# Products of the spectra in a long convolution: the order of two product pairs on VectorE, and of two spectrum stages on TensorE

## The chip, the cores and the metric

One Trainium2 chip, of which the kernel uses one core. Times are device microseconds of that core, as the median of several runs of the same kernel. A profile is one more execution, taken by the hardware profiler; its span runs from the first to the last instruction on the core.

## The reference

The program is a gated long convolution followed by two MLPs over 12480 tokens of 128 channels:

```python
u = x * v
L = 2 * S
Uf = np.fft.rfft(u, n=L, axis=1)
Hf = np.fft.rfft(h_filt, n=L, axis=0)
y = np.fft.irfft(Uf * Hf[None, :, :], n=L, axis=1)[:, :S, :]
return (x * y).astype(np.float32)
...
h = x @ w_in
g = np.where(h > 0.0, h, alpha * (np.exp(np.minimum(h, 0.0)) - 1.0))
return (g @ w_out).astype(np.float32)
...
h = x @ w_in
g = np.maximum(h, 0.0) + alpha * np.minimum(h, 0.0)
return (g @ w_out).astype(np.float32)
```

`h_filt` comes from a small MLP on position embeddings, times a decaying window. The change lies in `Uf * Hf`, the product of the two spectra.

## The kernel before, in words

The Fourier transforms are matrix products in two steps. The first (L239) leaves 99 residues of the input in `ureg` (view `a_u`) and of the filter in `sreg` (view `a_r`). The middle stage, the loop over `d` at L421 with 25 turns ("groups"; the program calls the group number d), finishes the transform of four residues a turn, multiplies the spectra and writes the products to DRAM (`yd`). Then comes the inverse transform (from L454 on) and the two MLPs, which take most of the time.

One group is made of these steps:
- `b_u(d)` (L337, TensorE): the spectrum of the input, 48 matmuls in the trace, into a PSUM tile of pool `psu` (name `pu`), which has two buffers. The products read it there, in PSUM.
- `b_h(d)` (L348, TensorE, 32 matmuls in the trace): the spectrum of the filter, from `rts[d % 2]`, into a tile of pool `psp` (name `ps`, two buffers). ScalarE copies it to SBUF (L351); that copy is `h`, two buffers.
- `b_r(d + 1)` (L319, TensorE, 32 matmuls): the residues of the next group's filter, also into a `psp` tile. ScalarE copies them to `rts[(d + 1) % 2]` with four copies (L323), which the next `b_h` reads.
- `products(d, u, h, 0, 2)` (L378). VectorE computes two large products of 128x1024, one for each pair of residues, e = 0 and e = 1 (L382); the small product `m2` of 128x512 for e = 1 (L385); the small product `mp` for e = 0, written over `u` in PSUM (L387); and the sum of `mp` into the tile of e = 0 (L388). GpSimd adds `m2` into the tile of e = 1 (L389) and then forms `y_sums`, two operations a pair (L371 and L372), first for e = 1, then for e = 0, into `ysts`. All five VectorE operations but L388 show at line L363, where `mul` stands.
- every second group, SyncE's queue writes the finished sums to DRAM (`y_write`, L400); each group it also loads the constants of the group three ahead (`load_g`, L271).

The large tiles come from `m_tile(True)` (L356): three slots of 1024 columns in `spreg`, taken in turn, so a group takes two and the slot that it takes first is the one after its predecessor's second. There is no scheduler: every engine runs its instructions in the order in which the program writes them, and waits for semaphores that the framework sets by tile regions. The last two groups, 23 and 24, compute only half of their products in the loop (`y1 == 1`) and the rest behind it (`late`, L440). Decoding of MLP weights (`dec_op`) is put between the groups by `run_hooks`: up to three extra VectorE operations of 128x512 a group, now and then one on ScalarE or GpSimd, in the first half of the loop only.

Of the kernel before, what the change touches and what calls it, by code (L numbers as in the profile page):

```python
# [13 lines left out]
ALU = mybir.AluOpType  # L14
# [32 lines left out]
def kernel(ctx: ExitStack, tc: tile.TileContext, posT, w1b, w2b, sc2, xva, xT,  # L47
                           fmat, fwin, gmat, wmat, finv, wi1, wo1, wi2, wo2, alphaT, out):
    nc = tc.nc
# [108 lines left out]
    def run_hooks(hooks, t):  # L158
        for x in sorted(hooks):
            if x <= t:  # L160
                for fn, args in hooks.pop(x):
                    fn(*args)
# [104 lines left out]
    def load_g(d):  # L267
        n = min(4, NF - 4 * d)
        o = 4096 + 4 * GWD * (d % 4)
        gts[d] = rreg[:, o : o + GWD * n].rearrange("p (f m) -> p f m", m=GWD)  # L270
        nc.sync.dma_start(gts[d], gmat[:, 4 * d : 4 * d + n, :])  # L271
# [32 lines left out]
    def fof(g, par):  # L304
        return min(2 * g + par, NF - 1)

    def rows(x):
        return slice(64 * x, 64 * x + 64)


    def b_r(d):
        ps = psp.tile([128, 1024], F32, name="ps")
        for e in range(2):
            for r in range(2):
                for par in range(2):
                    f = fof(2 * d + e, par)
                    for half in range(2):
                        c = par ^ half
                        nc.tensor.matmul(ps[rows(c), 512 * half + 128 * e : 512 * half + 128 * e + 128], a_r[rows(half), f, r],  # L319
                                         gts[d][rows(half), f - 4 * d, (64, 0)[r] : (192, 128)[r]], start=(r == 0), stop=(r == 1))  # L320
        for half in range(2):
            for par in range(2):
                nc.scalar.copy(rts[d % 2][rows(half), 256 * par : 256 * par + 256], ps[rows(par ^ half), 512 * half : 512 * half + 256])  # L323

    def b_u(d):
        ps = psu.tile([128, 1024], F32, name="pu")
        for e in range(2):
            for x in range(3):
                for par in range(2):
                    f = fof(2 * d + e, par)  # L330
                    for half in range(2):
                        o = 512 * half + 256 * e
                        a = a_u[rows(half), f]
                        src = (a.rearrange("k r w -> k (r w)"), a[:, 1], a[:, 0])[x]
                        dst = ps[rows(par), o + (0, 0, D)[x] : o + (2 * D, D, 2 * D)[x]]
                        g0 = (64, 0, 128)[x]
                        nc.tensor.matmul(dst, gts[d][rows(half), f - 4 * d, g0 : g0 + 64], src, start=(x == 0), stop=(x == 2))  # L337
        return ps.rearrange("k (h e r w) -> k h e r w", h=2, e=2, r=2)

    def b_h(d):  # L340
        ps = psp.tile([128, 1024], F32, name="ps")
        for e in range(2):
            for r in range(2):
                for par in range(2):
                    for half in range(2):
                        o = 512 * half + 256 * e + 128 * r
                        x = 256 * par + 128 * e + 64 * r
                        nc.tensor.matmul(ps[rows(par), o : o + D], rts[d % 2][rows(half), x : x + 64], w2_sb[rows(half)],  # L348
                                         start=True, stop=True)
        h = spreg[:, 4608 + 1024 * (d % 2) : 5632 + 1024 * (d % 2)]  # L350
        nc.scalar.copy(h.rearrange("k (e u w) -> k u e w", e=2, u=2), ps.rearrange("k (u e w) -> k u e w", u=2, e=2))  # L351
        return h.rearrange("k (e u r w) -> k e u r w", e=2, u=2, r=2)
# [3 lines left out]
    def m_tile(big):  # L356
        k = nm[big] % 3
        nm[big] += 1
        t = spreg[:, 1024 * k : 1024 * k + 1024] if big else spreg[:, 3072 + 512 * k : 3584 + 512 * k]
        return t.rearrange("k (r x w) -> k r x w", r=2, w=D)  # L360

    def mul(out, u, h, n):
        nc.vector.tensor_tensor(out, u.unsqueeze(2).to_broadcast([128, 2, n, D]), h.unsqueeze(1).to_broadcast([128, 2, n, D]), ALU.mult)  # L363

    def quarters(v):
        return v.rearrange("p y (h w) -> p y h w", h=NCH)

    def y_sums(g, m, y0, y1):
        q, e = divmod(g, 4)
        o = [ysts[q % 2][:, y0:y1, :, c, CH * e : CH * e + CH] for c in range(2)]  # L370
        nc.gpsimd.tensor_tensor(o[0], quarters(m[:, 0, 2 * y0 : 2 * y1 : 2]), quarters(m[:, 1, 2 * y0 + 1 : 2 * y1 : 2]), ALU.subtract)  # L371
        nc.gpsimd.tensor_tensor(o[1], quarters(m[:, 0, 2 * y0 + 1 : 2 * y1 : 2]), quarters(m[:, 1, 2 * y0 : 2 * y1 : 2]), ALU.add)  # L372

    def hx(h, e, u0, u1):
        return h[:, e, u0:u1].rearrange("k u r w -> k (u r) w")


    def products(d, u, h, y0, y1):  # L378
        n = 2 * (y1 - y0)
        ms = [m_tile(True) for e in range(2)]  # L380
        for e in range(2):
            mul(ms[e][:, :, 2 * y0 : 2 * y1], u[:, 0, e], hx(h, e, y0, y1), n)  # L382
        if y1 == 2:
            m2 = m_tile(False)
            mul(m2, u[:, 1, 1], hx(h, 1, 0, 1), 2)  # L385
            mp = u[:, 0].rearrange("k e r w -> k (e r w)").rearrange("k (r x w) -> k r x w", r=2, w=D)
            mul(mp, u[:, 1, 0], hx(h, 0, 0, 1), 2)  # L387
            nc.vector.tensor_tensor(ms[0][:, :, 2:4], ms[0][:, :, 2:4], mp, ALU.add)  # L388
            nc.gpsimd.tensor_tensor(ms[1][:, :, 2:4], ms[1][:, :, 2:4], m2, ALU.add)  # L389
        for e in (1, 0) if y1 == 2 else (0, 1):  # L390
            y_sums(2 * d + e, ms[e], y0, y1)

    def y_write(q, y0=0, y1=2):
        yst = ysts[q % 2][:, y0:y1].rearrange("p y h c w -> p (y h c) w")
        yv = yd[y0:y1].rearrange("y h (c k) w -> k (y h c) w", c=2)
        nfp = _fp_count(q)
        o = 8 * q * CH
        for par in range(2):
            nf = min(nfp, NF - 8 * q - nfp * par)
            nc.sync.dma_start(yv[:, :, o + par * nfp * CH : o + (par * nfp + nf) * CH],  # L400
                              yst[par * 64 : par * 64 + 64, :, : nf * CH])
# [19 lines left out]
    for d in range(ND):  # L421
        if d > 0 and d + 3 < ND:
            load_g(d + 3)
        run_hooks(hooks, 2 * d + 1)
        u = b_u(d)
        h = b_h(d)
        if d + 1 < ND:
            b_r(d + 1)
        if d > 1 and d % 2 == 0 and d < ND - 1:
            y_write(d // 2 - 1)  # L430
        if d < ND - 2:
            products(d, u, h, 0, 2)
        else:
            products(d, u, h, 0, 1)
            late.append((d, u, h))
# [4 lines left out]
    for d, u, h in late:  # L440
        products(d, u, h, 1, 2)
# [454 lines left out]
```

## Time and profile before

| | |
|---|---|
| time, median of 3 runs | 1517.39 us (1516.5 to 1523.01) |
| the profiled execution's own time | 1522.3 us |
| its span | 1520.5 us |
| TensorE matmul busy | 1430.0 us, 94% of the span |
| VectorE busy | 1282.5 us, 84% |
| ScalarE busy | 1087.5 us, 72% |
| GpSimd busy | 1019.3 us, 67% |
| mean granted TensorE clock | 0.985 of full speed |

The shares are means over stages with different limits. In the profile's forty slices of the span, TensorE's share is 9 tenths or more from the tenth slice (some 340 us) to the end and 6 to 8 tenths before it; the middle stage lies in the fourth to seventh slice, from about 117 to 277 us. PE means TensorE, PEld its weight loads, DVE VectorE, ACT ScalarE, POOL GpSimd, SP SyncE; the letter q behind a name is that engine's instruction queue.

### The profile page before, as it was taken

How to read it: one execution, taken by the hardware profiler on the slowest of the kernel's cores; microseconds unless marked ns; L12 is line 12 of the kernel's file. 1: busy time of each engine (PE TensorE's matmuls, PEld its weight loads, DVE VectorE, ACT ScalarE, POOL GpSimd, SP SyncE). 2: the span in 40 equal slices, each digit the busy share in tenths (PEclk: the TensorE clock that was granted, in tenths of full speed). 3: DMA queues.
4: the chain of work that ended last, by engine and by line, in shares of the span. 5: the costliest groups of instructions: out<-in, count | busy, mean ns of one | idle time of the engine just before them, and what ended most of it. 6: DMA issues, size and time to landing. Idle time of an engine off the chain costs nothing.

```text
span 1520.5 us, 25242 instructions
## 1 busy us (share of the span) xinstructions
PE 1430.0 (94%) x9143; PEld 1221.6 (80%) x9143; DVE 1282.5 (84%) x1817; ACT 1087.5 (72%) x2004; POOL 1019.3 (67%) x935
## 2 busy tenths in 40 slices
PE   7887666799999999999999999999999999999998
PEld 7886555788888888788888888888888888888887
DVE  5677776759898889888898898898888899988998
ACT  3444333467887777887888887878887888887884
POOL 4666776346678887888767666667666667666667
PEclk9999999899999999999999999999999999999999
DMA  8775687652012313222100400000000000000000
GB/s 257 222 259 143 158 236 197 200 160 82 19 45 59 87 49 87 69 76 83 50 8 18 195 25 24 24 7 18 24 24 24 25 7 17 25 24 21 7 7 13
DMA packets 98849, 116.89 MB, mean 77 GB/s; under 512 B 8518, under 2 KB 77834, under 8 KB 97560
## 3 DMA queue, kind: packets, MB, share of 16 engines
q1 hardware_dynamic: 95508, 104.19, 23.4%
q0 software_dynamic: 1296, 7.86, 1.5%
q10 hardware_dynamic: 1920, 3.21, 0.6%
q8 instruction: 72, 1.18, 0.3%
q14 instruction: 53, 0.43, 0.1%
HBM read 83.11 MB, written 32.15 MB: 76 GB/s over the span
## 4 chain that ended last, share of the span: by engine, by line
PE 67%; DVE 12%; POOL 8%; ACT 5%; issue 4%; DMA 4%; SPq 0%; POOLq 0%; ACTq 0%; DVEq 0%
PE psh L610 11%; PE psh L612 10%; PE psh L611 10%; PE pso L610 9%; PE pso L611 9%; PE pso L612 9%; PE psi L512 3%; DVE spreg L363 3%; DVE ureg L655 2%; PE pa L239 2%; POOL rreg L371 2%; POOL rreg L372 2%; POOL spreg L389 2%; PE ps L454 2%; DVE g1l L633 2%
## 5 line engine op out<-in xcount | busy, mean ns | idle before, releaser
L633 POOL TENSOR_TENSOR g2l<-ureg,g2h 128x490 fp32r<-128x490 f32 (+3 forms) x315 | 373.2, 1185 | 132.1 <-ACT g2h L684 63.5
L633 POOL TENSOR_TENSOR g1l<-ureg,g1h 128x486 fp32r<-128x486 f32 (+3 forms) x313 | 346.0, 1106 | 165.8 <-ACT g1h L661 159.7
L673 DVE TENSOR_SCALAR ureg<-psh,al_sb 128x486 f32<-128x486 f32 (+3 forms) x416 | 295.8, 711 | 83.7 <-PE psh L612 78.3
L647 ACT ACTIVATE ureg<-psh 128x490 f32<-128x490 f32 (+2 forms) x393 | 225.7, 574 | 114.1 <-PE psh L612 96.9
L678 DVE SCALAR_TENSOR_TENSOR ureg<-psh,ureg 128x486 f32<-128x486 f32 (+3 forms) x416 | 274.1, 659 | 14.3
L655 DVE SCALAR_TENSOR_TENSOR ureg<-ureg,psh 128x486 f32<-128x486 f32 (+3 forms) x416 | 268.1, 644 | 2.8 <-ACT ureg L648 2.0
L661 ACT CAST g1h<-ureg 128x490 fp32r<-128x490 f32 (+3 forms) x405 | 240.2, 593 | 17.8 <-DVE ureg L655 14.7
L648 ACT ACTIVATE ureg<-ureg 128x490 f32<-128x490 f32 (+2 forms) x393 | 239.7, 610 | 12.8
L684 ACT CAST g2h<-ureg 128x490 fp32r<-128x490 f32 (+3 forms) x404 | 234.6, 581 | 8.4 <-DVE ureg L678 6.8
L610 PE MATMUL psh<-x1h,wi1h 128*128 128x486 f32 (+3 forms) x416 | 169.7, 408 | 6.8 <-DVE ureg L655 3.9
L610 PE MATMUL psh<-x2h,wi2h 128*128 128x486 f32 (+3 forms) x416 | 158.6, 381 | 0.0
L611 PE MATMUL psh<-x2l,wi2h 128*128 128x486 f32 (+3 forms) x416 | 158.5, 381 | 0.0
L612 PE MATMUL psh<-x1h,wi1l 128*128 128x486 f32 (+3 forms) x416 | 158.3, 381 | 0.0
L612 PE MATMUL psh<-x2h,wi2l 128*128 128x486 f32 (+3 forms) x416 | 158.3, 381 | 0.0
L611 PE MATMUL psh<-x1l,wi1h 128*128 128x486 f32 (+3 forms) x416 | 158.2, 380 | 0.0
L611 PE MATMUL pso<-g2l,wo2h 128*128 128x490 f32 (+3 forms) x404 | 154.3, 382 | 0.6 <-POOL g2l L633 0.6
L610 PE MATMUL pso<-g1h,wo1h 128*128 128x490 f32 (+3 forms) x405 | 154.6, 382 | 0.3 <-ACT ureg L703 0.3
L611 PE MATMUL pso<-g1l,wo1h 128*128 128x490 f32 (+3 forms) x405 | 154.4, 381 | 0.2 <-POOL g1l L633 0.2
L612 PE MATMUL pso<-g1h,wo1l 128*128 128x490 f32 (+3 forms) x405 | 154.6, 382 | 0.0
L612 PE MATMUL pso<-g2h,wo2l 128*128 128x490 f32 (+3 forms) x404 | 154.1, 381 | 0.0
L610 PE MATMUL pso<-g2h,wo2h 128*128 128x490 f32 (+3 forms) x404 | 153.9, 381 | 0.0
L633 DVE TENSOR_TENSOR g1l<-ureg,g1h 128x490 fp32r<-128x490 f32 (+3 forms) x104 | 123.3, 1186 | 20.9 <-ACT g1h L661 10.3
(169 smaller groups left out, 2567.6 us busy)
## 6 DMA issues: line engine op xcount, KB each, us to landing
ureg<-yd SPq DMA_DIRECT2D x50, 256.0 KB
yd<-rreg SPq DMA_DIRECT2D x22, 512.0 KB
rreg<-in_gmat_dram SPq DMA_DIRECT2D x24, 384.0 KB
ureg<-in_finv_dram SPq DMA_DIRECT2D x23, 379.0 KB
ureg<-zd SPq DMA_DIRECT2D x4, 1584.0 KB
x<-in_xva_dram SPq DMA_DIRECT2D x32, 196.0 KB
v<-in_xva_dram SPq DMA_DIRECT2D x32, 196.0 KB
zd<-ureg SPq DMA_DIRECT2D x24, 256.0 KB
```

Of the source, the lines that this page charges most:

```text
L363: nc.vector.tensor_tensor(out, u.unsqueeze(2).to_broadcast([128, 2, n, D]), h.unsqueeze(1).to_broadcast([128, 2, n, D]), ALU.mult)
L610: nc.tensor.matmul(ps[:, :w], ah, bh[:, :w], start=start, stop=False)
L611: nc.tensor.matmul(ps[:, :w], ah, bl[:, :w], start=False, stop=False)
L612: nc.tensor.matmul(ps[:, :w], al, bh[:, :w], start=False, stop=stop)
L633: eng.tensor_tensor(lo[:, :w], e[:, :w], hi[:, :w], ALU.subtract)
L647: nc.scalar.activation(e[:, :w], ps[:, :w], AF.Relu, scale=-1.0)
L648: nc.scalar.activation(e[:, :w], e[:, :w], AF.Exp, scale=-1.0)
L655: nc.vector.scalar_tensor_tensor(e[:, :w], e[:, :w], -1.0, ps[:, :w], op0=ALU.add, op1=ALU.max)
L661: nc.scalar.copy(hi[:, :w], e[:, :w])
L673: nc.vector.tensor_scalar(e[:, :w], ps[:, :w], 0.0, al_sb[:, c : c + 1], op0=ALU.min, op1=ALU.mult)
L678: nc.vector.scalar_tensor_tensor(e[:, :w], ps[:, :w], 0.0, e[:, :w], op0=ALU.max, op1=ALU.add)
L684: nc.scalar.copy(hi[:, :w], e[:, :w])
```

## The change

Two things are written in another order; no operation is added or removed, and none changes its size.

```diff
     def products(d, u, h, y0, y1):
         n = 2 * (y1 - y0)
-        ms = [m_tile(True) for e in range(2)]
-        for e in range(2):
+        ms = {}
+
+        def first(e):
+            ms[e] = m_tile(True)
             mul(ms[e][:, :, 2 * y0 : 2 * y1], u[:, 0, e], hx(h, e, y0, y1), n)
+
+        first(1)
         if y1 == 2:
             m2 = m_tile(False)
             mul(m2, u[:, 1, 1], hx(h, 1, 0, 1), 2)
+            nc.gpsimd.tensor_tensor(ms[1][:, :, 2:4], ms[1][:, :, 2:4], m2, ALU.add)
+        y_sums(2 * d + 1, ms[1], y0, y1)
+        first(0)
+        if y1 == 2:
             mp = u[:, 0].rearrange("k e r w -> k (e r w)").rearrange("k (r x w) -> k r x w", r=2, w=D)
             mul(mp, u[:, 1, 0], hx(h, 0, 0, 1), 2)
             nc.vector.tensor_tensor(ms[0][:, :, 2:4], ms[0][:, :, 2:4], mp, ALU.add)
-            nc.gpsimd.tensor_tensor(ms[1][:, :, 2:4], ms[1][:, :, 2:4], m2, ALU.add)
-        for e in (1, 0) if y1 == 2 else (0, 1):
-            y_sums(2 * d + e, ms[e], y0, y1)
+        y_sums(2 * d, ms[0], y0, y1)
...
         run_hooks(hooks, 2 * d + 1)
+        h = b_h(d)
         u = b_u(d)
-        h = b_h(d)
         if d + 1 < ND:
             b_r(d + 1)
```

Since `m_tile` is now called for e = 1 first, the slots change hands too: the first slot of a group holds e = 1, the second e = 0.

On VectorE, the first two groups of the loop before (the two large products, x2, are e = 0 and e = 1; then `m2`, `mp` and the sum):

```order
L363 TENSOR_TENSOR spreg<-pu,spreg 128x1024 x2
L363 TENSOR_TENSOR spreg<-pu,spreg 128x512
L363 TENSOR_TENSOR pu<-pu,spreg 128x512
L388 TENSOR_TENSOR spreg<-spreg,pu 128x2x256
L363 TENSOR_TENSOR spreg<-pu,spreg 128x1024 x2
L363 TENSOR_TENSOR spreg<-pu,spreg 128x512
L363 TENSOR_TENSOR pu<-pu,spreg 128x512
L388 TENSOR_TENSOR spreg<-spreg,pu 128x2x256
```

and the same place in the changed kernel:

```order
L363 TENSOR_TENSOR spreg<-pu,spreg 128x1024
L363 TENSOR_TENSOR spreg<-pu,spreg 128x512
L363 TENSOR_TENSOR spreg<-pu,spreg 128x1024
L363 TENSOR_TENSOR pu<-pu,spreg 128x512
L396 TENSOR_TENSOR spreg<-spreg,pu 128x2x256
L363 TENSOR_TENSOR spreg<-pu,spreg 128x1024
L363 TENSOR_TENSOR spreg<-pu,spreg 128x512
L363 TENSOR_TENSOR spreg<-pu,spreg 128x1024
L363 TENSOR_TENSOR pu<-pu,spreg 128x512
L396 TENSOR_TENSOR spreg<-spreg,pu 128x2x256
```

The large product of e = 0 has moved behind `m2`; the rest stands as before.

On TensorE, from `b_r(0)` at the loop's entry through group 1 before (L337 is `b_u`, L348 `b_h`, L319 `b_r`; each row's matmul counts twice in the trace):

```order
L319 MATMUL ps<-rreg,sreg 64x128 x16
L337 MATMUL pu<-ureg,rreg 64x256 x4
L337 MATMUL pu<-ureg,rreg 64x128 x8
L337 MATMUL pu<-ureg,rreg 64x256 x4
L337 MATMUL pu<-ureg,rreg 64x128 x8
L348 MATMUL ps<-w_sb,rreg 64x128 x16
L319 MATMUL ps<-rreg,sreg 64x128 x16
L337 MATMUL pu<-ureg,rreg 64x256 x4
L337 MATMUL pu<-ureg,rreg 64x128 x8
L337 MATMUL pu<-ureg,rreg 64x256 x4
L337 MATMUL pu<-ureg,rreg 64x128 x8
L348 MATMUL ps<-w_sb,rreg 64x128 x16
```

and in the changed kernel:

```order
L319 MATMUL ps<-rreg,sreg 64x128 x16
L348 MATMUL ps<-w_sb,rreg 64x128 x16
L337 MATMUL pu<-ureg,rreg 64x256 x4
L337 MATMUL pu<-ureg,rreg 64x128 x8
L337 MATMUL pu<-ureg,rreg 64x256 x4
L337 MATMUL pu<-ureg,rreg 64x128 x8
L319 MATMUL ps<-rreg,sreg 64x128 x16
L348 MATMUL ps<-w_sb,rreg 64x128 x16
L337 MATMUL pu<-ureg,rreg 64x256 x4
L337 MATMUL pu<-ureg,rreg 64x128 x8
L337 MATMUL pu<-ureg,rreg 64x256 x4
L337 MATMUL pu<-ureg,rreg 64x128 x8
```

`b_h` now follows `b_r` directly, where `b_u` stood between them. ScalarE, GpSimd and SyncE's queue keep their order, but for the two half groups 23 and 24, whose sums GpSimd now forms for e = 1 first.

## Rows read from the trace of the kernel before

**Rows 1.** Windows: start and end, length, busy of five engines (instructions), clock, DMA share, GB/s.

```profile
117.00:262.00 145.00, 96.67 (x2548) 82.72 (x2552) 108.15 (x128) 59.24 (x124) 101.63 (x119) 0.91 0.69 183
...
300.00:1520.00 1220.00, 1207.79 (x5692) 1020.25 (x5691) 1072.61 (x1535) 964.17 (x1775) 842.57 (x744) 1.00 0.14 45
```

**Rows 2.** Chain that ended last, one group of the loop: start us, us, what.

```profile
251.30 1.83 DVE spreg L363 x2
253.27 1.28 POOL spreg L389
254.61 0.73 POOL rreg L371
256.71 0.70 POOL rreg L372
```

**Rows 3.** Timeline, VectorE and GpSimd: start, us, operation [idle before <- releaser].

```profile
251.30 1.82 DVE L363 TENSOR_TENSOR spreg<-pu,spreg 128x1024 f32<-128x1024 f32 x2 [1.72 <-POOL rreg L372]
...
253.16 0.70 DVE L363 TENSOR_TENSOR pu<-pu,spreg 128x512 f32<-128x512 f32 x1
253.27 1.27 POOL L389 TENSOR_TENSOR spreg<-spreg 128x512 f32<-128x512 f32 x1 [2.00 <-DVE spreg L363]
253.89 0.69 DVE L388 TENSOR_TENSOR spreg<-spreg,pu 128x512 f32<-128x512 f32 x1
254.50 1.22 DVE L363 TENSOR_TENSOR spreg<-pu,spreg 128x1024 f32<-128x1024 f32 x1
...
257.43 1.82 DVE L363 TENSOR_TENSOR spreg<-pu,spreg 128x1024 f32<-128x1024 f32 x2 [1.72 <-POOL rreg L372]
```

**Rows 4.** Timeline, TensorE and ScalarE, in the same group.

```profile
254.63 1.97 PE L337 MATMUL pu<-ureg,rreg 64*64 64x256 f32 x48 [2.42 <-DVE spreg L388]
...
256.42 1.05 PE L348 MATMUL ps<-w_sb,rreg 64*64 64x128 f32 x32
...
257.29 1.05 PE L319 MATMUL ps<-rreg,sreg 64*64 64x128 f32 x32
...
257.58 1.01 ACT L351 COPY spreg<-ps 128x1024 f32<-128x1024 f32 x1 [3.68 <-PE ps L348]
258.49 1.54 ACT L323 COPY rreg<-ps 64x256 f32<-64x256 f32 x4
```

**Rows 5.** Timeline, group 1: `b_h` behind ScalarE's four copies, then `b_r`.

```profile
117.35 1.54 ACT L323 COPY rreg<-ps 64x256 f32<-64x256 f32 x4
...
117.77 0.43 PE L348 MATMUL ps<-w_sb,rreg 64*64 64x128 f32 x2 [0.78 <-ACT rreg L323]
118.55 1.36 PE L348 MATMUL ps<-w_sb,rreg 64*64 64x128 f32 x29 [0.36 <-ACT rreg L323]
...
119.66 0.33 PE L319 MATMUL ps<-rreg,sreg 64*64 64x128 f32 x3
```

**Rows 6.** Timeline of TensorE around a fall of the clock; the fifth row is of the windows.

```profile
180.07 3.69 PE L337 MATMUL pu<-ureg,rreg 64*64 64x256 f32 x48 [3.03 <-DVE spreg L388]
...
183.53 1.93 PE L348 MATMUL ps<-w_sb,rreg 64*64 64x128 f32 x32
...
230.11 3.57 PE L337 MATMUL pu<-ureg,rreg 64*64 64x256 f32 x48 [2.42 <-DVE spreg L388]
233.44 1.19 PE L348 MATMUL ps<-w_sb,rreg 64*64 64x128 f32 x32
...
182.00:184.00 2.00, 2.00 (x40) 1.63 (x36) 0.71 (x1) 0.00 (x0) 1.25 (x2) 0.50 0.00 0
...
153.79 1.97 PE L337 MATMUL pu<-ureg,rreg 64*64 64x256 f32 x48 [3.22 <-DVE spreg L388]
```

**Rows 7.** Timeline: the first products of group 0 and of group 24.

```profile
117.54 2.95 DVE L363 TENSOR_TENSOR spreg<-pu,spreg 128x1024 f32<-128x1024 f32 x3 [1.29 <-ACT spreg L351]
...
266.46 3.08 DVE L363 TENSOR_TENSOR spreg<-pu,spreg 128x512 f32<-128x512 f32 x5 [2.22 <-ACT spreg L351]
```

**Rows 8.** Windows: the stretch of the loop in which the DMA engines are fullest.

```profile
184.00:216.00 32.00, 24.50 (x620) 21.13 (x612) 22.57 (x27) 13.31 (x28) 22.76 (x27) 0.86 0.94 255
```

## The prediction

> **What bounds the kernel now.** I read the windows first, to see which stage can gain. From 300 us on TensorE is busy 1207.79 of 1220 us: that part is full, and the change does not touch it. In the loop over the groups no engine is full: in 145 us VectorE works 108.15, GpSimd 101.63, TensorE 96.67 and ScalarE 59.24 [rows 1]. A stage in which nobody is full is held by a circle of waits, so the chain comes next. It goes round once a group: two VectorE products, GpSimd's L389, its four sums (of which the chain's rows show the outer two), and back to the products [rows 2]. The next turn begins at 257.43 [rows 3], 6.13 us after 251.30.
>
> The timeline says what closes the circle [rows 3]. VectorE runs the large product of e = 0 early (254.50), then idles 1.72 us until GpSimd's last L372 is done, and only then runs the large product of e = 1 and `m2` (257.43). That is the rotation of three slots: e = 1 takes the slot in which the group before had its e = 0, and GpSimd sums e = 0 last. GpSimd for its part idles 2.00 us for `m2`, which stands behind the blocked product. The sum along the circle: 1.83 for e = 1 and `m2`, 0.14 to GpSimd's start at 253.27, 1.34 to the first sum at 254.61, 2.82 for four sums: 6.13.
>
> TensorE and ScalarE lie beside this [rows 4]: `b_u` waits 2.42 us for VectorE to free its PSUM buffer, then `b_u`, `b_h`, `b_r` run through. The spectra are ready well before VectorE takes them.
>
> **The change, part by part.** *The products.* The group's first slot now holds e = 1, and its `m2` follows at once. The slot that e = 1 takes was last summed two groups earlier; the one that e = 0 takes held the e = 1 of the group before, which GpSimd sums first. So GpSimd's last sums are off VectorE's path. What is left is the work alone. VectorE: from 251.30 to the next group's e = 0 at 254.50 is 3.20, plus 1.15 for that product (1.22 less the overlap of consecutive rows): 4.35 us a group. GpSimd: from 253.27 to 257.42, 4.15 us [rows 3]. Nothing is added or lengthened: every GpSimd L389 and L371 here already runs beside VectorE's products. In the first half of the loop the decoding adds twelve operations of 128x512 on VectorE and six on GpSimd; at the 0.70 and 1.27 us of such operations here, 8 us over twelve groups on either, some 0.7 a group: 5.0 and 4.8 us.
>
> *The exchange of `b_h` and `b_u`.* This is what now sets the pace, I think. Before, `b_u(d+1)` stood between `b_r(d+1)` and `b_h(d+1)`, and covered ScalarE's four copies L323. Now `b_h` follows `b_r` directly and must wait for those copies; behind it on TensorE's queue wait `b_u` and the next `b_r`, and VectorE waits for `b_u`. A new circle: copies, `b_h`, `b_u`, `b_r`, copies. Its price is in the rows. Group 1 shows `b_h` behind the copies: its first two matmuls start at 117.77, the bulk from 118.55 with a last wait inside, and `b_r` follows at 119.66, that is 2.31 us after the copies began [rows 5]. From `b_u` to its successor 1.79, `b_r` 1.05, and 0.11 from TensorE's end to ScalarE's start (256.42 plus 1.05 to 257.58) [rows 4]: together 5.26. The bulk of that `b_r` started a tenth later; I take 5.3 us a group. ScalarE's L351 fits beside `b_u`, and `h` (copied while `b_u` runs) is ready before `u`. So the pace goes from 6.13 to 5.3, set by TensorE and ScalarE, not to VectorE's 4.35.
>
> *Where it begins and ends.* The copies of group 1 begin at 117.35 [rows 5] in both kernels: ScalarE's first L351 waits for transfers out of the memory that it overwrites. Group 24's copies then begin 23 x 5.3 = 121.9 us later, at 239.3; add 2.3 for `b_h`, 1.97 for `b_u` and a tenth: VectorE takes group 24 at 243.7, against 266.46 [rows 7]. That is **22.8 us** earlier. It counts the decoding's delays of today, which the slack of VectorE and GpSimd now swallows, and that group 24 no longer waits for `b_h` and L351 behind `b_u`. What comes behind (sums, write, load, inverse transform) keeps its order, and the full TensorE of the MLPs passes the gain on.
>
> *The clock.* Today a fall of the granted clock is free here; on the new circle it is not. Seven of the 23 `b_u` that begin between 121 and 261 us are long ones of 2.95 to 3.69 us, as at 180.07, where the row of windows grants 0.50, the 1.2 GHz level. All seven follow an idle gap of at least 2.42 us, but so do nine that stay at 1.97, one behind 3.22; none falls behind 1.10 or less [rows 6]. The new circle has a gap of about 1.7 us a group (copies and signals), which this trace does not show. Price of one fall: at 230.11 the successor starts 3.33 us later instead of 1.79, 1.5 us; at 180.07 it is 1.67 plus 0.88 on `b_h`, 2.55 us [rows 4, 6]; I take 2. Number of falls: from none to seven, as now; the gaps are shorter, so I take three, nearer to none. That takes 6 us: a gain of **16.8 us**.
>
> Edits costed at nothing: the half groups' order of pairs and the late products, which TensorE's and the DMA's work on the loop's end covers; without that cover, one half pair of sums, under 1 us. SyncE's queue keeps its order, and `load_g` still goes out some three groups ahead.
>
> The profiled execution took 1522.3 us, of which 1520.5 is span; less 16.8 is 1505.5. The median of the runs lies 4.9 below that execution, so I say 1500.6.
>
> **The rivals.**
> *A, the clock falls in most groups: slower.* TensorE is now on the path, with a gap in every group. If its clock falls in 20 of 23 groups, that costs 40 us against 22.8: 1517.4 + 17.2 = 1535. The gain is gone at 11 falls; from 15 or 16 on it is slower by 0.5%. For it: the gap recurs at each turn and a fall lengthens the very circle. Against it: the gaps are shorter than any that fell today, and TensorE's 3.7 us a group (1.79, 0.87 and 1.05) become a larger share of a shorter turn. A rule for it stands in the Trainium skill (TensorE: Matmul & The Clock Gate, A second HAM failure mode: psum-queue depth-cycling): a matmul engine that idles briefly between groups while PSUM buffers go round can swing between the two clock levels and lose throughput to it. By that rule the time would be this rival's; the trace agrees only in part, as gaps of 2.42 us fell in some groups and not in others. Chance 0.06.
>
> *B, the DMA engines hold part of it: smaller or no gain.* From 184 to 216 us they are 0.94 full [rows 8]. If those five groups keep their 6.13, 4 us are lost; if groups 11 to 24 all do, 14 x 0.83 = 11.6 us, which with the clock's three falls leaves a gain of 5: 1512. For it: the same bytes must pass in less time. Against it: over the loop the share is 0.69 [rows 1], 0.69 x 6.13 / 5.3 = 0.80, and loads go out three groups ahead. Chance of a gain under 7.6 us this way, or of a wait for GpSimd that stays (the slots not freed as I read them, then 1517): 0.09.
>
> *C, the new circle does not close* and VectorE's 4.35 sets the pace: 22 more us, 1478. Against it: `b_h` waits for ScalarE in group 1 already [rows 5]. Chance 0.04.
>
> **How the numbers follow.** My forecast, a gain of 8 to 23 us, has 0.81, C 0.04: faster by over 0.5% (7.6 us, about what a measurement of this kernel can tell from no change) 0.85; same 0.09; slower 0.06. The range: no fall and all of the 22.8 gives 1494.6, with a little for the pace 1493; seven falls of 2 us and 2 us of DMA waits leave 6.8, so 1510.6. 1493 to 1511.
>
> **What would show it.** In the changed kernel's trace: VectorE's and GpSimd's waits on each other nearly gone, VectorE's wait for `b_u` (L337) in their place; turns of 5.2 to 5.4 us at full clock, one or two us longer where the clock falls; TensorE's wait before L348 on ScalarE's L323; group 24 at about 244 to 252 us. I am wrong if VectorE still waits for L372, if turns of 5.3 do not appear at full clock, or if the clock is 0.50 in most groups.

## The result, and the profile after

The changed kernel takes 1499.79 us, the median of 4 runs (1498.55 to 1500.85), against 1518.72 us for the kernel before beside it (1516.50 to 1523.01). The ratio is 0.9871 (95% interval 0.9855 to 0.9887): 1.3% faster, clear of what the runs scatter. The forecast was 1500.6. Its profiled execution has a span of 1499.0 us, 21.5 less than the one before.

The time came from the loop over the groups, in which five engines now stand like this (windows: start and end, length, busy of PE, PEld, DVE, ACT and POOL with instructions, clock, DMA share, GB/s), beside [rows 1] and [rows 8]:

```profile
117.00:240.00 123.00, 101.85 (x2512) 83.00 (x2508) 105.10 (x124) 58.11 (x115) 100.13 (x119) 1.00 0.80 215
182.00:224.00 42.00, 34.94 (x860) 28.35 (x864) 32.18 (x38) 18.38 (x36) 32.32 (x40) 1.00 0.95 277
```

The clock is at its full level throughout the loop, where it was 0.91 of it on the mean, and the DMA engines' share went from 0.69 to 0.80. VectorE and GpSimd in the timeline of the changed kernel (start, us, operation, [idle before <- releaser]), which answers to [rows 3]:

```profile
224.43 2.95 DVE L363 TENSOR_TENSOR spreg<-pu,spreg 128x1024 f32<-128x1024 f32 x3 [1.00 <-PE pu L337]
...
226.33 1.27 POOL L390 TENSOR_TENSOR spreg<-spreg 128x512 f32<-128x512 f32 x1 [1.25 <-DVE spreg L363]
...
229.76 0.72 POOL L372 TENSOR_TENSOR rreg<-spreg 128x256 f32<-128x256 f32 x1
229.84 2.95 DVE L363 TENSOR_TENSOR spreg<-pu,spreg 128x1024 f32<-128x1024 f32 x3 [1.01 <-PE pu L337]
```

A turn lasts 5.41 us (224.43 to 229.84) instead of 6.13. VectorE runs its three products without a break and no longer waits for GpSimd's L372, which is still running when VectorE starts (229.76 and 229.84); it waits 1 us for `b_u` (L337). TensorE and ScalarE in the same turn answer to [rows 4]:

```profile
225.29 1.54 ACT L323 COPY rreg<-ps 64x256 f32<-64x256 f32 x4 [1.64 <-PE ps L319]
...
225.71 0.43 PE L348 MATMUL ps<-w_sb,rreg 64*64 64x128 f32 x2 [0.54 <-ACT rreg L323]
...
226.50 1.36 PE L348 MATMUL ps<-w_sb,rreg 64*64 64x128 f32 x29 [0.36 <-ACT rreg L323]
...
227.60 0.39 PE L337 MATMUL pu<-ureg,rreg 64*64 64x256 f32 x3
...
227.81 1.79 PE L337 MATMUL pu<-ureg,rreg 64*64 64x256 f32 x44
...
228.05 1.01 ACT L351 COPY spreg<-ps 128x1024 f32<-128x1024 f32 x1 [1.22 <-issue]
...
229.34 0.33 PE L319 MATMUL ps<-rreg,sreg 64*64 64x128 f32 x3
229.44 0.27 PE L337 MATMUL pu<-ureg,rreg 64*64 64x128 f32 x1
229.44 1.14 PE L319 MATMUL ps<-rreg,sreg 64*64 64x128 f32 x29
...
230.71 1.54 ACT L323 COPY rreg<-ps 64x256 f32<-64x256 f32 x4 [1.64 <-PE ps L319]
```

Read from top to bottom this is the circle: copies, `b_h` behind them, `b_u`, `b_r`, and the next copies 5.42 us later. The totals of waits from 117 to 240 us (engine, line <- whom: us, times, longest) say the same of the whole loop:

```profile
ACT rreg L323 <- PE ps L319: 38.1, 22, 2.4
PEld ps L348 <- ACT rreg L323: 34.7, 66, 0.8
...
DVE spreg L363 <- PE pu L337: 14.1, 14, 1.5
...
DVE spreg L363 <- POOL rreg L372: 1.8, 1, 1.8
```

The circle keeps its 5.41 us through the turns with decoding as well. VectorE's own turns there are up to 6.87 us long; it falls behind, catches up in later turns of down to 4.32 us, and does not hold TensorE.

Four turns were longer. In them TensorE stopped inside `b_r`, `b_h` or `b_u`, at an instruction for which the profile names no releaser, as here, where the copies came 6.2 us after the last ones:

```profile
136.27 0.66 PE L319 MATMUL ps<-rreg,sreg 64*64 64x128 f32 x14 [0.59 <-issue]
...
137.03 1.54 ACT L323 COPY rreg<-ps 64x256 f32<-64x256 f32 x4 [2.43 <-PE ps L319]
```

The others are at 199, 212 and 218 us. Together they cost 2.5 us. A second profiled execution of the changed kernel (`e8_change_again`, below) has none of them: its copies follow each other by 5.40 to 5.46 us in all 23 turns, with the DMA engines as full as here:

```profile
117.00:240.00 123.00, 102.88 (x2569) 84.89 (x2572) 106.87 (x127) 58.72 (x117) 102.04 (x120) 1.00 0.80 219
```

So full DMA engines alone do not make these stops. The profile's list of DMA queues (packets, MB, share) has a queue that, by its name, loads the engines' own code:

```profile
q8 instruction: 72, 1.18, 0.3%
```

In the packets that the trace keeps, each of the four stops ends 1.4 to 1.6 us after one of this queue's 16 KB packets was done (here 134.79, and 136.27 for the stop's end). The same holds for every such stop of 0.18 us or more in the loops of all twelve profiles of this case: 30 stops in six of them, 1.27 to 1.63 us after such a packet, while the packets come 3 to 13 us apart. That TensorE waited there for its own code is the reading that fits; no run changed the code's loading, so the cause is not shown.

The chain at the loop's end, in order of time:

```profile
246.08 0.70 DVE spreg L363
...
249.19 2.44 DMA yd<-rreg
...
251.84 2.87 DMA sreg<-yd
...
254.84 6.62 PE ps L460 x32
```

VectorE takes group 24 at 246.08, where it was 266.46 [rows 7], 20.4 us earlier. Eight to nine microseconds later the inverse transform begins, at 254.84; in the profile before it began at 275.26, the same 20.4. So the end of the loop and the MLPs passed on what they were given.

### The profile page after: what moved, and what is told of

Read it like the earlier page. It is cut to its first block, busy times and chain, and to the rows that moved or that the text cites. A ratio compares the mean times of both kernels' runs of the same rounds, so it can differ in the third digit from the quotient of the medians.

```text
span 1499.0 us, 25227 instructions
## 1 busy us (share of the span) xinstructions
PE 1432.3 (96%) x9143; PEld 1217.6 (81%) x9143; DVE 1279.1 (85%) x1817; ACT 1089.8 (73%) x2004; POOL 1019.6 (68%) x935
## 4 chain that ended last, share of the span: by engine, by line
PE 67%; DVE 8%; ACT 4%; issue 3%; POOL 1%; DMA 1%; POOLq 0%; SPq 0%; ACTq 0%; DVEq 0%
PE psh L616 11%; PE psh L618 10%; PE psh L617 10%; PE pso L616 10%; PE pso L617 10%; PE pso L618 10%; PE psi L518 3%; DVE ureg L661 2%; PE ps L460 2%; DVE g1l L639 2%; DVE ureg L679 1%; PE pu L460 1%; DVE ureg L684 1%; DVE g2l L639 1%; ACT ureg L654 1%
## 5 line engine op out<-in xcount | busy, mean ns | idle before, releaser
L667 ACT CAST g1h<-ureg 128x490 fp32r<-128x490 f32 (+3 forms) x405 | 240.3, 593 | 17.6 <-DVE ureg L661 14.1
```

The lines of the kernel that those rows point to most:

```text
L667: nc.scalar.copy(hi[:, :w], e[:, :w])
```

## The experiments

Every kernel ran beside the kernel before on its chip; ratios are to that. Three things were in question: whether the new circle sets the pace, what the exchange of `b_h` and `b_u` does, and which part of the products' new order opened the old circle.

**The products alone** (`e1_products_alone`): the change without its second part.

```diff
-        h = b_h(d)
         u = b_u(d)
+        h = b_h(d)
```

> Only the new order of the products, with b_u still ahead of b_h. Theory (the exchange makes the circle of copies, b_h, b_u, b_r that sets 5.41 us a turn in the changed kernel): without it VectorE's own 4.35 us sets the pace, about 5.0 while the decoding runs, so some 23 x 0.7 = 16 us less than the changed kernel, 1478 to 1490; VectorE's waits in the loop nearly gone. Rival (the exchange is needed, because b_u and b_h behind VectorE's free buffer bring h too late, above all where the clock falls): turns of 5.4 us or more, 1500 to 1515, with VectorE waiting for L351 in most groups.

Measured: 1490.6 us, ratio 0.9814 (0.9779 to 0.985). A second time, in one job with the changed kernel:

> The products alone once more. Theory (the exchange costs time): 6 to 12 us under the changed kernel beside it, 1488 to 1495. Rival (the first difference was the chip's): within 3 us of it.

> The changed kernel once more, beside the next two on one chip. Theory and rival alike: 1498 to 1504. Its profile tells whether the clock stays up in the loop in another execution: theory, no fall or one, since a turn of 5.41 us leaves short gaps; rival, falls come and go by chance, three or more.

Measured: 1493.09 us, 0.9828 (0.9811 to 0.9845), against 1498.6 us, 0.9860 (0.9843 to 0.9876), for the changed kernel. So the products alone are some 5 us better than the whole change beside it, and 9 by the medians of separate jobs; the intervals of the pair touch. The theory's direction holds and its size does not: the range of 1478 to 1490 was missed at its upper end, and beside the changed kernel the difference is 5.5 us where 6 to 12 were expected. The changed kernel's clock stayed at the full level in its second profile too, as the theory had it. The first profile of the products alone tells what took the rest. Its timeline:

```profile
118.48 2.94 DVE L363 TENSOR_TENSOR spreg<-pu,spreg 128x1024 f32<-128x1024 f32 x3
122.80 2.94 DVE L363 TENSOR_TENSOR spreg<-pu,spreg 128x1024 f32<-128x1024 f32 x3
...
131.77 2.94 DVE L363 TENSOR_TENSOR spreg<-pu,spreg 128x1024 f32<-128x1024 f32 x3
...
137.18 0.91 POOL L371 TENSOR_TENSOR rreg<-spreg 128x256 f32<-128x256 f32 x1
...
137.54 1.10 DVE L129 SCALAR_TENSOR_TENSOR ureg<-ureg 128x512 uint32<-128x512 uint32 x1
...
138.57 2.94 DVE L363 TENSOR_TENSOR spreg<-pu,spreg 128x1024 f32<-128x1024 f32 x3
...
198.70 1.10 PE L319 MATMUL ps<-rreg,sreg 64*64 64x128 f32 x32 [1.19 <-DMA rreg<-in_gmat_dram]
...
203.91 0.76 PE L348 MATMUL ps<-w_sb,rreg 64*64 64x128 f32 x18 [1.94 <-issue]
...
205.99 2.96 DVE L363 TENSOR_TENSOR spreg<-pu,spreg 128x1024 f32<-128x1024 f32 x3 [2.89 <-ACT spreg L351]
```

Without the exchange a bare turn (one without decoding) is 4.32 us (118.48 to 122.80), as VectorE's work asks: the exchange does cost 1.1 us a turn where nothing else is in the way. But VectorE's 22 turns from group 0 to group 22 take 109.8 us (`mp` starts at 117.15 and at 226.99), 14.8 more than 22 x 4.32. Of these, 8.9 lie in the turns with decoding, up to 177.86: one reaches 6.8 us (131.77 to 138.57), with VectorE busy all through it. Those turns are as long in the changed kernel, within 0.1 us, so the exchange costs nothing in them. The other 5.9 us lie behind: there `b_r` waits 1.7 us in all for the constants of its group, as at 198.70, and VectorE's longest wait, 2.89 us, goes back to a stop of 1.94 us inside `b_h` (203.91), one of those that end shortly after a packet of code (1.27 us). The row of windows there:

```profile
180.00:212.00 32.00, 25.03 (x704) 21.48 (x700) 26.38 (x32) 14.87 (x32) 27.41 (x35) 1.00 0.99 299
```

The DMA engines are at 0.99 (0.95 in the second profile). Full transfers, of data and of code, are the likely bound of this stretch when the circle is cut; that is argued from the share and these waits, not shown.

**`b_r` ahead of `b_u`** (`e3_b_r_before_b_u`): another way to cut the circle, with `b_h` still first.

```diff
         h = b_h(d)
-        u = b_u(d)
         if d + 1 < ND:
             b_r(d + 1)
+        u = b_u(d)
```

> The changed products, and on TensorE b_h(d), b_r(d+1), b_u(d): ScalarE's four copies then run while b_u does (1.54 against 1.79 us). Theory: the circle is cut, the pace is VectorE's, 4.4 us and about 5.0 with the decoding: 1478 to 1490, much like the products alone. Rival (the DMA engines are the next bound: they are 0.80 busy in the changed kernel's loop and 0.94 and more from 184 to 224 us): groups from 12 on stay at 5.2 us or more and b_r or the sums wait for transfers: 1492 to 1500.

Measured: 1497.52 us, 0.9841 (0.9813 to 0.9869). The rival holds in its time and its waits; of its turns only the mean is 5.2 us or more from group 12 on (5.3 from copies to copies). Bare turns are 4.32 us here too (VectorE, 186.97 to 191.29), so the circle is cut, but TensorE now asks for each group's constants earlier. The totals of waits from 117 to 240 us:

```profile
PE ps L319 <- DMA rreg<-in_gmat_dram: 15.4, 8, 3.8
```

Its row of windows for the same stretch:

```profile
117.00:240.00 123.00, 95.95 (x2514) 85.99 (x2506) 106.51 (x130) 56.66 (x115) 104.04 (x126) 0.92 0.84 226
```

Eight times, 15.4 us in all, TensorE waited for transfers, and the clock fell again (0.92).

**The loads spread** (`e7_loads_spread`): the products alone, with the loads of the finished sums further apart.

```diff
-        for i, x in enumerate(((24, 25, 26, 28)[k], 35 + k, 44 + k)):
+        for i, x in enumerate(((23, 27, 31, 35)[k], 36 + 2 * k, 44 + k)):
```

> The products alone (b_u ahead of b_h), with the first eight loads of the finished sums spread over turns 11 to 21 where they went out in turns 12 to 14 and 17 to 19. Theory (without the exchange the loop is held by crowded transfers between 180 and 210 us, where b_r and the sums wait for them): some 5 us less than the products alone, 1482 to 1487. Rival (the DMA engines are full all the same, 0.82 over the loop): 1488 to 1493.

Measured: 1490.15 us, 0.9809 (0.9783 to 0.9835), the same as the products alone. The waits moved (3.60 us for L351 at 210.57 is the longest) and did not go. Which transfer would have to be smaller was not tried.

**The exchange alone** (`e2_exchange_alone`): `b_h` ahead of `b_u`, products as before.

```diff
-        u = b_u(d)
         h = b_h(d)
+        u = b_u(d)
```

> Only b_h ahead of b_u, products as before. Theory (the circle through GpSimd's last sums holds the loop): turns stay at 6.13 us, VectorE still waits for L372; only the loop's end gains some 2 us, since group 24 no longer waits for b_h and the copy of h behind b_u: 1513 to 1519. Rival (the exchange brings a good part of the gain by itself): 1500 to 1510.

Measured: 1516.99 us, 0.9983 (0.9965 to 1.0). VectorE's rows show the old circle whole, at 6.14 us a turn:

```profile
241.83 1.82 DVE L363 TENSOR_TENSOR spreg<-pu,spreg 128x1024 f32<-128x1024 f32 x2 [1.73 <-POOL rreg L372]
...
247.97 1.82 DVE L363 TENSOR_TENSOR spreg<-pu,spreg 128x1024 f32<-128x1024 f32 x2 [1.74 <-POOL rreg L372]
```

The exchange by itself brings at most 0.35%, which these runs cannot tell from nothing.

**The slots alone** (`e4_slots_alone`): the exchange, and of the products' order only that e = 1 takes its slot first.

```diff
-        ms = [m_tile(True) for e in range(2)]
+        ms = {e: m_tile(True) for e in (1, 0)}
```

> The exchange, and of the products only the slots: e = 1 takes its slot first, while VectorE computes e = 0, e = 1, m2, mp as before. Theory (the slot that e = 1 waited for is what closed the circle; m2's earlier place is of no use): the same pace as the changed kernel, 5.41 us, 1498 to 1503. Rival (m2 must come early so that GpSimd's 4.15 us fit into the turn): turns of 5.7 us or more, 1507 to 1515.

Measured: 1511.95 us, 0.9941 (0.9925 to 0.9958). The rival holds: `m2`'s early place is about half of the matter. The timeline shows a smaller circle in place of the old one:

```profile
224.01 2.95 DVE L363 TENSOR_TENSOR spreg<-pu,spreg 128x1024 f32<-128x1024 f32 x3 [1.43 <-POOL rreg L372]
...
227.04 1.27 POOL L389 TENSOR_TENSOR spreg<-spreg 128x512 f32<-128x512 f32 x1 [1.69 <-DVE spreg L363]
...
228.39 0.73 POOL L371 TENSOR_TENSOR rreg<-spreg 128x256 f32<-128x256 f32 x1
...
229.07 0.74 POOL L372 TENSOR_TENSOR rreg<-spreg 128x256 f32<-128x256 f32 x1
...
229.84 2.95 DVE L363 TENSOR_TENSOR spreg<-pu,spreg 128x1024 f32<-128x1024 f32 x3 [1.42 <-POOL rreg L372]
```

The slot that is free first is now wanted by e = 0, VectorE's first product of a turn, and GpSimd frees it only after `m2`, VectorE's third. So all three products (2.95), L389 and one pair of sums stand in a row: 5.83 us. In the change e = 0 is the third product, and GpSimd is done with the slot by then.

**Longer copies, in both kernels** (`e5_copies_longer_after`, `e6_copies_longer_before`): ScalarE makes the second pair of copies twice.

```diff
-        for half in range(2):
+        for half in (0, 1, 1):
             for par in range(2):
                 nc.scalar.copy(rts[d % 2][rows(half), ...
```

> The changed kernel with six copies L323 a group in place of four (the second pair is made twice, with the same result), 0.77 us more of ScalarE's time. Theory (copies, b_h, b_u, b_r in one circle): every turn grows by 0.77 to 6.18 us, 23 x 0.77 = 17.7 us: 1515 to 1520. Rival (ScalarE has slack, as its 58 busy us of 123 suggest, and something else sets the turn): under 5 us more, 1498 to 1505.

> The kernel before with the same six copies. Theory (with b_u between b_r and b_h, and the turn set by the sums, the copies are covered): no more than 2 us, 1516 to 1524. Rival (they are on the path there too): 15 us or more, 1532 and up.

Measured: 1533.07 us, 1.0091 (1.0066 to 1.0117), on the changed kernel, some 33 us more than without; 1518.36 us, 0.9984 (0.9968 to 1.0001), on the kernel before, nothing. So the copies are on the path after the change and covered before it, and the rival with slack on ScalarE falls. But 33 is nearly twice what 0.77 us a turn can give. The timeline of the first (VectorE, GpSimd and TensorE, in two groups of rows):

```profile
216.53 2.95 DVE L363 TENSOR_TENSOR spreg<-pu,spreg 128x1024 f32<-128x1024 f32 x3 [1.72 <-POOL rreg L372]
224.31 2.95 DVE L363 TENSOR_TENSOR spreg<-pu,spreg 128x1024 f32<-128x1024 f32 x3 [3.37 <-PE pu L337]
229.61 0.73 POOL L372 TENSOR_TENSOR rreg<-spreg 128x256 f32<-128x256 f32 x1
230.43 2.95 DVE L363 TENSOR_TENSOR spreg<-pu,spreg 128x1024 f32<-128x1024 f32 x3 [1.72 <-POOL rreg L372]
...
219.31 2.14 PE L348 MATMUL ps<-w_sb,rreg 64*64 64x128 f32 x29 [1.12 <-ACT rreg L323]
...
227.08 1.36 PE L348 MATMUL ps<-w_sb,rreg 64*64 64x128 f32 x29 [1.12 <-ACT rreg L323]
...
230.02 0.27 PE L337 MATMUL pu<-ureg,rreg 64*64 64x128 f32 x1
```

Two of its windows, a fall of the clock inside a turn and the loop:

```profile
220.00:222.00 2.00, 2.00 (x37) 1.82 (x33) 0.91 (x2) 0.30 (x1) 2.00 (x4) 0.50 0.04 8
117.00:240.00 123.00, 93.89 (x2016) 78.50 (x2016) 87.27 (x104) 60.37 (x131) 82.05 (x96) 0.89 0.69 182
```

Turns are of two kinds: 6.12 us at full clock (224.31 to 230.43), as foretold within a tenth, and 7.6 to 7.8 us where the granted clock falls to 0.50, its 1.2 GHz level, inside the turn (216.53 to 224.31). Ten of the loop's turns are of the second kind. Ten times 1.6 us and 23 times 0.7 make 32 us.

That the full-clock turns come near the old circle's 6.13, and that the profile names L372 at their start, does not bring the old circle back. L372 only ended last, at 230.34, 0.05 us behind `b_u`'s last matmul (230.02 and 0.27: 230.29). VectorE starts 0.14 us after that matmul; in the changed kernel it starts 0.13 after it (229.71 and 229.84) with L372 still running. From copies to copies the turn is 6.13 us (225.11 to 231.24), through `b_h`, `b_u` and `b_r` as before.

**The exchange for the last two groups only** (`e10_exchange_at_the_end`):

```diff
+        if d >= ND - 2:
+            h = b_h(d)
         u = b_u(d)
-        h = b_h(d)
+        if d < ND - 2:
+            h = b_h(d)
```

> The products, with b_h ahead of b_u for groups 23 and 24 only. Theory (inside the loop the exchange costs 1 us a turn, at its end it spares VectorE the wait for b_h and the copy of h): 1 to 3 us under the products alone. Rival (the end is held by transfers): the same as the products alone within 1 us.

Measured: 1494.11 us, 0.9829 (0.9814 to 0.9843), the same as the products alone beside it. The theory fails: VectorE waits 3.00 us before group 23 and 4.10 before group 24, now for `b_u`, which stands behind `b_h` and its copies; in the products alone beside it, it waited 2.95 us before group 24, for L351, and not before group 23. The waits grew by 4 us, and the 22 turns before them happened to be 3.4 us shorter in this profile (108.2 us against 111.6), so the equal times do not speak for the rival either: it is not transfers that VectorE waits for here.

## Why the prediction was right

**The old circle and its opening: right.** VectorE's wait for L372 is gone. One of 1.8 us still bears its name, but ends 0.14 us after `b_u`'s last matmul (212.97 and 213.11), like the others. The exchange alone changes nothing and the products alone give more than the whole gain, so the products' order is the cause. One step was told too simply: the prediction let the slots do it. The slots with the exchange give less than half of the change's gain (0.9941 against 0.9871); the early `m2` is needed with them.

**The new circle as the pace: right, a little short.** The change was to run at 5.3 us a turn and runs at 5.41. Of the sum's three legs, from the copies to what follows `b_h` came out at 2.31, as reckoned (225.29 to 227.60), and `b_u` at 1.74 for 1.79 (to 229.34). The last, `b_r` and the signal to ScalarE, took 1.37 for 1.16 (to 230.71): `b_r` begins while `b_u`'s last matmul is still to come, and lasts 1.24 us from its first matmul, not 1.05. Over 23 turns the missing 0.11 is 2.5 us. Making the copies longer moved the turn by 0.7 after the change and not at all before it, and taking them out of the circle brought the turn to 4.32, the 4.35 that was reckoned for VectorE. The circle is shown, not only argued. Its starting point was a little off too: ScalarE's first L351 does not wait for transfers in the changed kernel, but runs right behind `b_h` at 111.97, and group 1's copies come 5.36 us after group 0's (5.66 before).

**The clock: mis-sized, to the good.** Three falls at 2 us were charged; there were none in the loop, in two profiled executions of the changed kernel. That term was 6 us and came out as 0.

**The held turns: 2.5 us in one profile, nothing in the other.** The sum had no term for them. Three of the four lie in the stretch from 182 to 224 us where the DMA engines' share is 0.95; but the second profile has 0.94 there and no turn held, so the share alone is not the cause. The packets of code fit better (above); the cause stays open.

**The sum.** 22.8 less 2.5 for the pace and 2.5 for the held turns is 17.8. From the copies of group 1 to VectorE's group 24 it was 149.1 us before (117.35 to 266.46) and is 131.5 now (114.57 to 246.08): 17.6. So the forecast of 16.8 for the loop was right as a sum of terms that were off by 6 and 5 the other way, and that it came so close is in part luck. In the second profile of the changed kernel, without held turns, the same stretch is 129.0 us (116.16 to 245.16) and the gain 20.1. Luck, too, is in the last step: the median was taken 4.9 us under the profiled execution, and in the changed kernel it lies 1.1 under it (1499.79 and 1500.85). The medians side by side differ by 18.9, the spans by 21.5. The profiles before and after differ by 2.8 us more at the loop's start; the first `b_r`, which stands ahead of everything changed, began between 105.92 and 114.49 us in the profiles of these kernels, so 2.5 of the 2.8 (110.50 and 108.02) is scatter of the stage before.

**The rivals.** A (the clock falls in most turns, slower) did not come, but it was near: with ScalarE's copies half as long again the kernel is slower than before, for that reason. B (the DMA engines) did not come: their share rose to 0.80 as reckoned, and in the second profile groups 11 to 24 kept the circle's pace. C (the circle does not close) is what the products alone look like, and its 1478 was out of reach: 1490.6 and 1493.09 were measured. Its price took 4.35 us for every turn and left out the decoding, which the prediction itself had put at 8 us for VectorE and which took 8.9, some operations 1.10 us beside GpSimd instead of 0.70; the waits behind 180 us took another 5.9.

## What to carry to other kernels

When no engine of a stage is full, find the circle of waits, open it, and then ask at once which circle or which full queue is next: here it was a circle that the same change had closed, with the copies between two matmul stages. Keep an independent piece of work between a matmul stage and the stage that needs its copied result; the exchange took that piece away and cost 1.1 us of a bare turn. And before leaving a circle that runs through TensorE, look at its idle gap: here copies 0.77 us longer brought the clock down in ten turns and nearly doubled the damage, 33 us for 17.7.

## What the runs showed of the hardware

The changed kernel's granted clock stayed at the full level through the 23 turns of the loop, in both profiles; in each turn TensorE waited twice for the copies, 0.54 and 0.36 us by its matmul rows. With longer copies, waits of 0.49 and 1.12 us and turns of 6.12 us, it fell to the 1.2 GHz level in ten turns, each then 1.5 to 1.7 us longer. The Trainium skill (TensorE: Matmul & The Clock Gate, A second HAM failure mode: psum-queue depth-cycling) tells of such swinging in a kernel that idles briefly between groups of matmuls; the trace with the longer copies agrees, and the changed kernel's, with the shorter waits, shows none.

VectorE's decoding operations, with all operands in SBUF, take longer beside GpSimd: L129 takes 1.10 us beside it (137.54 in the products alone) and 0.69 with GpSimd idle, as before the changed kernel's loop:

```profile
111.43 0.69 DVE L129 SCALAR_TENSOR_TENSOR rreg<-rreg 128x512 uint32<-128x512 uint32 x1
```

GpSimd's L371 takes 0.91 beside it instead of 0.73. The products, which read one operand from PSUM, keep their length beside it (0.70 for 128x512 in every profile). The Trainium skill (SBUF — State Buffer, SBUF: two separate sides) says that VectorE and GpSimd exclude each other at one shared pair of SBUF ports, for VectorE operations with two SBUF inputs among others; the rows agree that those operations are among the ones that take longer.
